# Causal attention and an ELU FFN on one core: first queries of later pairs in float16, and new planner costs

## The chip, the cores and the metric

The kernel runs on one core of a Trainium2 chip. The metric is the device time of one execution in microseconds (us), the median of several runs. The core has five engines with queues of their own: PE (TensorE: matmuls; its weight loads are shown as PEld), DVE (VectorE), ACT (ScalarE), POOL (GpSimd) and SP (SyncE), which here only issues DMAs. Each engine takes its instructions in order. Data lie in SBUF (128 partitions), in PSUM (where PE writes, eight banks) and in DRAM.

## The reference

Attention over 8 batches, 8 heads, 576 positions and 64 dimensions per head, causal, with a decay bias; then a two-layer FFN from 512 over 2048 to 512 with an ELU:

```python
scores = q @ k.T / 8
cum = cumsum(maximum(s, 0))                     # per batch and head
bias = minimum(-(cum[:, None] - cum[None, :]), 0)
scores = where(causal, -1e9, scores + bias)
attn = softmax(scores)                          # with + 1e-9 in the divisor
x = (attn @ v), heads side by side              # 4608 x 512, float32
h = x @ w_in
g = where(h > 0, h, exp(minimum(h, 0)) - 1)
out = g @ w_out                                 # 4608 x 512, float32
```

q, k and v arrive in float32. The two weight matrices arrive as 8-byte floats and are decoded on the chip.

## The kernel before, in words

**A planner.** Nothing is issued in the order in which the code is written. Each step is handed to `op` as a list of ways (engine, cost in ns, the call) with what it reads and writes and a priority. `Plan.issue` then simulates the engines with these costs: again and again it takes the step that could start first (ties go to the lower priority number), on the engine where it would end first, and appends it to that engine's queue. What comes of it is one fixed order for each engine. A load is planned on SP and is taken to land after a transfer time (bytes by `RATE`) and a fixed `LAG`, 4000 ns. `MARGIN` is added where PE depends on another engine. Up to 130 us of planned time the costs and margins are those of the early stage, then the steady ones (`STEADY_T`, `STEADY_BIAS`, `STEADY_MARGIN`). `W0` and `WD` set the priority of the weight units among the attention units: weight unit f has 25 + 3f, the attention units go up in steps of 10 and 5.

**Fillers.** While planned PE time is below `FILL_T` (60 us), gaps of PE are filled with turns of the identity matrix into a scratch bank (line 1556). Nothing reads it. A "turn" is a transposition of a 128x128 tile on PE.

**Attention, first batches.** The first three batches' first 320 positions are computed in float32 by `Low` units, one for each pair of heads (12 units; lines 756 to 895). The two heads' first 64 queries share one 128-row tile (`pair`); the other blocks follow. Probabilities are turned on PE (lines 851 and 867), copied to SBUF, and multiplied with v (lines 853 and 882) into one bank. The pair's product gives 64 rows with 128 columns, one half of them for each head; so the bank is emptied by one copy of 256 columns and two copies of 64 columns that move a head's half to its partitions. Then x goes to DRAM.

**Attention, later pairs.** All other positions use float16 in two parts, high and low (three products instead of one). In five batches each of the four head pairs has a unit with `h is None` for the 64 first queries of both heads, 20 in all, followed by one unit per head. Scores (line 1074) go through DVE with the mask (line 1077) and ACT's Exp (line 1082). For the head units, the normalized probabilities are split into float16 parts (`halved`, lines 1134 to 1142) and turned by a transposing DMA on SP (`turned_load`, line 418). For the first queries the tile stays float32: it is normalized (lines 1095 to 1099), turned on PE (line 1227), evicted into two fp32r parts by a copy and a subtraction (`split_pt`, lines 452 and 1160) and multiplied with an fp32r split of v (line 1220). Four operations (`halves`, lines 452 and 1289) add the diagonal blocks and bring them into x. The heads' products (line 1261) run on halves of the array, one for each head, and are scaled on the way out (lines 1273 and 1275).

**Scales.** Powers of two for the float16 parts come from maxima over all partitions: the per-partition maxima are multiplied with the identity (line 667), reduced on DVE, and spread again by a product with ones (line 670). That happens 13 times.

**FFN.** The 4608 rows of x are taken in 18 chunks of 256. Chunk 0 is computed in float32 (lines 1432 and 1486) while weights arrive; the others use float16 parts (lines 1436 and 1493). A weight unit is a 512 KB load into one of four raw buffers (line 413), an operation on ACT for its high words (line 702), one on DVE or ACT for its low words (lines 706 and 708), one on DVE that joins them (line 711), and a maximum (line 632 or 635). When all 32 are there, the scales are formed and the weights are split (lines 437 to 439 and 726). FFN steps have the priority number 10000 and more on PE, so they fill what attention leaves.

Of the kernel before, what the change touches and what calls it, by code (L numbers as in the profile page):

```python
# [9 lines left out]
F32 = mybir.dt.float32  # L10
F32R = mybir.dt.float32r
# [24 lines left out]
LAG, RATE = 4000.0, 285.0  # L36
W0, WD = 25, 3
# [14 lines left out]
FILL_T, GAP = 60e3, 350.0  # L52
# [44 lines left out]
class Plan:  # L97
# [17 lines left out]
    MARGIN = {"PE": 100.0}  # L115
    STEADY_MARGIN = {"PE": 500.0}

# [82 lines left out]
    def issue(self):  # L200
# [19 lines left out]
        while pending:  # L220
# [144 lines left out]
def kernel(  # L365
# [55 lines left out]
    def rounded(prio, n, dst, src, reads, writes, sign=1.0, only=None):  # L421

        ways = [
            ("Pool", pool_1(n),
             lambda: pool.tensor_scalar(dst(), src(), sign, 1.0, ALU.mult, ALU.mult)),
            ("ACT", act_s(n),
             lambda: act.activation(dst(), src(), AF.Copy, scale=sign)),
            ("DVE-SB", dve_1(n),
             lambda: dve.tensor_scalar(dst(), src(), sign, None, ALU.mult)),
        ]  # L430
        op(prio, [w for w in ways if only is None or w[0] in only], reads, writes)

# [9 lines left out]
    def rest(prio, n, dst, src, hi, reads, writes, only=None):  # L442

        ways = [
            ("DVE-SB", dve_2(n), lambda: dve.tensor_tensor(dst(), src(), hi(), ALU.subtract)),
            ("Pool", pool_2(n), lambda: pool.tensor_tensor(dst(), src(), hi(), ALU.subtract)),
        ]
        op(prio, [w for w in ways if only is None or w[0] in only], reads, writes)
# [36 lines left out]
    def decay_sums():  # L485
# [25 lines left out]
        op(-10, [("DVE-SB", 4390.0, first)], [], [(aux, "row"), (k_first, "sums")])  # L511
# [103 lines left out]

    def scale_tiles():
# [29 lines left out]
    def scales_of(prio, spans, dst):  # L646
# [20 lines left out]
        op(prio, [("PE", pe4(P), lambda: pe_.matmul(flat.v[:, :P], tops.v, ident, start=True, stop=True))],  # L667
# [17 lines left out]
    def load_unit(f, kind, src):  # L685
# [4 lines left out]
        if wide:  # L690
            slot = (2 * f + kind) % N_RAW

            def raw(t):
# [15 lines left out]
                    raw(0), raw(0), AF.Copy, scale=7.49 * 2.0**-32)),  # L709
            ], [], [(raws, (slot, 0))])  # L710
# [131 lines left out]
    def weighing_low(u):  # L842
# [6 lines left out]
        def pair():  # L849
            tr = plan.buf(ps, [P, 512], F32, f"trl_{u.tag}", tag="a", bufs=N_A)  # L850
            op(prio, [("PE", 111.0, lambda: pe_.transpose(tr.v[:, :P], u.first.v, ident))], [u.first], [tr])
            psum_copy(prio, P, lambda: turned.v[:, :P], lambda: tr.v[:, :P], [tr], [(turned, "pair")])
            op(prio, [("PE", pe4(P), lambda: pe_.matmul(
                av.v[:HB, n : n + P], u.vs.v[:, 0], turned.v[:, :P], start=True, stop=True))],
               [(turned, "pair"), u.vs], [av])

        def keys(kb):
# [22 lines left out]
            def products():  # L880
                for h in range(2):
                    pe_.matmul(av.v[h * HB : (h + 1) * HB, n - c : n], u.vs.v[:, 1 + 2 * kb + h], dst()[:, h],
# [147 lines left out]
    def prepare(u):  # L1030
# [17 lines left out]
        src, used = (lambda: u.va.v[:, j, :1]), values_of(u.va, j)  # L1048
# [108 lines left out]
    def split_pt(prio, tag, tr, w):  # L1157
        pc = plan.buf(sb, [P, 2, w], F32R, f"pc_{tag}", tag="pc")
        psum_copy(prio, w, lambda: pc.v[:, 0], lambda: tr.v[:, :w], [tr], [(pc, 0)])
        op(prio, [("DVE", dve_p(w), lambda: dve.tensor_tensor(  # L1160
            pc.v[:, 1], tr.v[:, :w], pc.v[:, 0].bitcast(F32), ALU.subtract))],
           [tr, (pc, 0)], [(pc, 1)])
        return [(pc, 0), (pc, 1)]

    def scoring(u):
# [8 lines left out]
        if u.h is None:  # L1174
            sm = plan.buf(sb, [P, 1], F32, f"sm_{u.tag}", tag="sm", bufs=2)
            psh = u.pp = plan.buf(sb, [P, P], F32, f"psh_{u.tag}", tag="pc")

            def pair():
# [6 lines left out]
                    (sm, 0, True, 1, 1.0), view=lambda v: v.rearrange("p (h t) -> p h t", h=2),  # L1185
                )
                normalize(prio, psh, P, sm, 0)
# [24 lines left out]
    def weighing(u):  # L1212

        prio = u.prio + 1
        av = plan.buf(ps, [P, 512], F32, f"av_{u.tag}", tag="av", bufs=N_AV)

        def products(cost, pairs, dst, first, last):

            for m, (reads, operands) in enumerate(pairs):
                op(prio, [("PE", cost, lambda m=m, operands=operands: pe_.matmul(  # L1220
                    av.v[:, dst], *operands(), start=first and m == 0,
                    stop=last and m == len(pairs) - 1))], reads, [av])
# [439 lines left out]
```

## Time and profile before

| | us |
|---|---|
| three runs | 1029.07, 1031.0, 1031.82 |
| median | 1031.0 |
| profiled execution | 1028.56 |
| its span | 1026.4 |

The span runs from the first to the last instruction of the profile. In what follows, a row of the group view names a line, an engine, an operation, what it writes and reads, its shape and count; then come busy time in us and mean ns of one, then the idle time of the engine before them and what ended it. Rows of the timeline begin with start and duration in us. Matmuls overlap: a row's duration is longer than the distance to the next matmul's start. Rows of the window view show busy us and count of each engine in a stretch, the granted clock of PE, the busy share of the 16 DMA engines and GB/s. `_None` at the end of a tile's name marks the units of the first queries of later pairs; names that end in `l` (`trl`, `avl`, `xl`) belong to the first batches.

### The profile page before, as it was taken

The numbers are of one execution on the slowest core, as the hardware profiler recorded it, in microseconds if no ns is written. First come the engines' busy times: TensorE is split into PE (matmuls) and PEld (weight loads), VectorE is DVE, ScalarE is ACT, GpSimd is POOL, SyncE is SP. The second block draws the span as 40 slices with busy tenths as digits, with TensorE's granted clock in tenths as the row PEclk, the third lists the DMA queues.
The fourth block names the chain that finished last, engine by engine and source line by source line (L and its number), as shares of the span: only waits on it lengthen the run. The fifth ranks groups of instructions, "written<-read, shape, count | busy, mean of one in ns | idle before, by whom it ended". The sixth has DMA issues, their size and how long they took to land. (4 is left out here: it accounts for less than half of the span.)

```text
span 1026.4 us, 21904 instructions
## 1 busy us (share of the span) xinstructions
PE 1005.4 (98%) x7342; PEld 690.3 (67%) x7342; DVE 851.8 (83%) x2394; ACT 661.5 (64%) x1583; POOL 247.0 (24%) x411
## 2 busy tenths in 40 slices
PE   8899999999999999999999999999999999999998
PEld 7666656776666666666666666667666766666665
DVE  6898899888989988889999999898879898763343
ACT  5888746667767777667676777765757666553232
POOL 6231432233232122212422322131212132100000
PEclk9999999999999999999999999999999999999999
DMA  7898324689989998879999999989987998851000
GB/s 204 261 281 258 98 83 129 147 184 238 207 180 190 215 214 186 168 186 230 189 188 207 217 192 192 212 194 202 218 186 178 218 214 177 166 109 48 1 22 21
DMA packets 296725, 179.85 MB, mean 175 GB/s; under 512 B 209908, under 2 KB 270564, under 8 KB 296612
## 3 DMA queue, kind: packets, MB, share of 16 engines
q1 hardware_dynamic: 296612, 178.45, 77.2%
q8 instruction: 58, 0.95, 0.4%
q14 instruction: 55, 0.45, 0.2%
HBM read 93.08 MB, written 36.81 MB: 127 GB/s over the span
## 5 line engine op out<-in xcount | busy, mean ns | idle before, releaser
L1436 PE MATMUL h<-xh,wp 128*128 128x256 f16 x2176 | 398.6, 273 | 0.0
L1493 PE MATMUL o<-wp,gg 128*128 128x512 f16 x1632 | 392.6, 379 | 1.0 <-DVE gg L1475 1.0
L1436 PEld LDWEIGHTS <-wp 128*128 128x128 f16 x3264 | 317.2, 98 | 65.2 <-issue 2.4
L1436 PE MATMUL h<-xl,wp 128*128 128x256 f16 x1088 | 296.5, 273 | 0.7 <-DVE xl L1412 0.7
L1493 PEld LDWEIGHTS <-gg 128*128 128x128 f16 x1632 | 157.9, 98 | 147.1 <-DVE gg L1475 2.9
L1082 ACT ACTIVATE p<-p,mn 128x192 f32<-128x192 f32 (+1 forms) x232 | 143.9, 620 | 65.5 <-DVE mn L1077 59.9
L1142 DVE SCALAR_TENSOR_TENSOR p<-p,sm,p 128x512 f16<-128x512 f32 (+3 forms) x263 | 158.6, 622 | 1.3 <-POOL p L1134 0.3
L1448 ACT ACTIVATE g<-h,cs 128x512 f32<-128x512 f32 x136 | 92.4, 680 | 84.3 <-PE h L1436 83.9
L1472 ACT ACTIVATE gg<-h 128x512 f16<-128x512 f32 x134 | 79.6, 594 | 89.3 <-DVE h L1468 87.8
L1077 DVE CUSTOM_DVE_ANT_0 p<-sc,maskw 128x192 f32<-128x192 f32 (+1 forms) x232 | 109.0, 480 | 11.0 <-PE sc L1074 8.9
L1074 PE MATMUL sc<-set 128*128 128x288 f16 (+3 forms) x544 | 110.8, 298 | 3.3 <-DVE mn L1077 3.2
L1475 DVE SCALAR_TENSOR_TENSOR gg<-h,gg 128x512 f16<-128x512 f32 x136 | 93.2, 686 | 22.8 <-ACT gg L1472 22.1
L1134 POOL TENSOR_SCALAR p<-p,sm 128x64 f16<-128x64 f32 (+3 forms) x77 | 54.2, 707 | 225.9 <-DVE sm L1088 88.8
L1468 DVE SCALAR_TENSOR_TENSOR h<-g,cs,h 128x512 f32<-128x512 f32 x136 | 101.9, 749 | 5.5 <-ACT g L1455 1.4
L1138 ACT ACTIVATE p<-p,sm 128x512 f16<-128x512 f32 (+3 forms) x147 | 78.6, 545 | 18.4 <-ACT p L1082 6.6
L1459 DVE TENSOR_SCALAR g<-g 128x512 f32<-128x512 f32 x98 | 43.2, 441 | 55.2 <-ACT g L1448 54.8
L1074 PEld LDWEIGHTS <-set 128*128 128x128 f16 x584 | 54.7, 98 | 37.8 <-issue 6.0
L1261 PEld LDWEIGHTS <-v 128*64 128x64 f16 x960 | 48.2, 110 | 21.3 <-issue 11.9
L1261 PE MATMUL av<-T,v 128*64 128x256 f16 (+5 forms) x960 | 61.4, 278 | 0.8 <-DMA T<-p 0.8
L437 POOL TENSOR_SCALAR v<-va,scales 128x320 f16<-128x320 f32 (+1 forms) x35 | 24.2, 691 | 115.2 <-PE av L1261 92.7
L437 POOL TENSOR_SCALAR xh<-xc,cs 128x512 f16<-128x512 f32 x23 | 17.3, 753 | 112.8 <-PE h L1436 104.6
L1082 ACT ACTIVATION_READ_ACCUMULATOR p<-p,mn 128x1 f32 x232 | 43.6, 188 | 0.0
(202 smaller groups left out, 1264.0 us busy)
## 6 DMA issues: line engine op xcount, KB each, us to landing
set<-spread SPq DMA_DIRECT2D x32, 432.0 KB
spread<-parts_None SPq DMA_DIRECT2D x32, 288.0 KB
set<-spread SPq DMA_DIRECT2D x32, 288.0 KB
raws<-in_w_in_dram SPq DMA_DIRECT2D x16, 512.0 KB
raws<-in_w_out_dram SPq DMA_DIRECT2D x16, 512.0 KB
out_dram<-ost SPq DMA_DIRECT2D x32, 256.0 KB
va<-in_vb_dram SPq DMA_DIRECT2D x16, 352.0 KB
xc<-x_dram SPq DMA_DIRECT2D x22, 256.0 KB
```

The source lines that it names most:

```text
L1074: pe_.matmul(view(sc.v[:, :cw]), l, r, start=n == 0, stop=n == len(pairs) - 1)
L1077: op(prio, [("DVE", 168 + cw + 55 * (i > 0), lambda i=i, sc=sc: dve.tensor_tensor_reduce(pt.v[:, i * cw : (i + 1) * cw], sc.v[:, :cw], mv( ...
L1082: op(prio, [("ACT", 383 + w / 1.2, lambda: act.activation(pt.v[:, :w], pt.v[:, :w], AF.Exp, bias=mn.v[:, n - 1 : n], scale=-1.0, accum_out ...
L1138: ("ACT", 295 + size / 1.2, lambda part=part: act.activation(part(0), own(part), AF.Copy, scale=sm.v[:, r])),
L1142: ("DVE-SB", dve_2(size), lambda part=part: dve.scalar_tensor_tensor(part(1), own(part), sm.v[:, r], part(0), ALU.mult, ALU.subtract)),
L1261: pe_.matmul(av.v[w.h * HB : (w.h + 1) * HB, dst], w.values.v[:, w.h, kb, v], part(w, kb, m), start=kb == 0 and m == 0 and v == 0, stop=kb ...
L1436: pe_.matmul(columns(k), weight_part(f, 0, part)[1]()[:, c * P : (c + 1) * P], xx.v[:, c], start=(c == 0 and m == 0), stop=(c == NCB - 1 a ...
L1448: op(side, [("ACT", act_c(W) + (0 if native else 90), lambda: act.activation(g.v, hp.v, AF.Exp, scale=1.0 if native else by(3)))], [hp] + ...
L1468: op(side, [("DVE", dve_p(W) + 60, lambda: dve.scalar_tensor_tensor(hp.v, g.v, by(2 if sign[0] else 1), hp.v, ALU.mult, ALU.max))], [g, cs ...
L1472: ("ACT", act_c(W), lambda: act.activation(gg.v[:, 0], hp.v, AF.Copy, scale=2.0**-DOWN)),
L1475: op(side, [("DVE", dve_p(W), lambda: dve.scalar_tensor_tensor(gg.v[:, 1], hp.v, 2.0**-DOWN, gg.v[:, 0], ALU.mult, ALU.subtract))], [hp, ( ...
L1493: pe_.matmul(acc[i].v, gg.v[:, g, at], weight_part(f, 1, part)[1](), start=(f == 0 and m == 0), stop=(f == NF - 1 and m == 2),)
```

## The change

Later pairs' first queries: the probabilities are scaled by 2^15 over their sum and split into two float16 parts (`split_scaled`: a scaled copy on POOL, ACT or DVE, then the remainder on DVE), and both parts go through one transposing DMA of two blocks. The values of these queries are split into float16 parts as well. The products are six matmuls of 64 columns, one head on each half of the array; they stand in `heads` of the pair's second head, ahead of its products, share its bank and eviction where these fit in 512 columns (batch 3), and have a bank and an eviction of 64 columns of their own elsewhere.

First batches: the pair's product is made for each head on its half of the array, with 64 columns, so that the bank is emptied by one copy of 320 columns. The decoding of low words may also run on POOL. The scales' turns use the transposition of PE. An Exp on ACT is added near the start. Planner values change: `LAG` is 2300 plus 300 early and 1700 later, `W0` 22, the early margin of PE 50, `FILL_T` 42 us, and the first scan's cost 3100 ns.

```diff
-LAG, RATE = 4000.0, 285.0
-W0, WD = 25, 3
+LAG, RATE = 2300.0, 285.0
+W0, WD = 22, 3
-FILL_T, GAP = 60e3, 350.0
+FILL_T, GAP = 42000.0, 350.0
...
-    MARGIN = {"PE": 100.0}
+    MARGIN = {"PE": 50.0}
     STEADY_MARGIN = {"PE": 500.0}
+    EARLY_LAG, STEADY_LAG = 300.0, 1700.0
...
-                lag = pipe + o.ways[n][3] - end
+                lag = pipe + o.ways[n][3] + (self.STEADY_LAG if steady else self.EARLY_LAG) - end
...
+    def split_scaled(prio, n, dst, src, by, used, parts):
+        scaled(prio, n, lambda: dst(0), src, by, used, [(parts, 0)])
+        op(prio, [("DVE-SB", dve_2(n), lambda: dve.scalar_tensor_tensor(
+            dst(1), src(), by(), dst(0), ALU.mult, ALU.subtract))], [*used, (parts, 0)], [(parts, 1)])
...
-        op(-10, [("DVE-SB", 4390.0, first)], [], [(aux, "row"), (k_first, "sums")])
+        op(-10, [("DVE-SB", 3100.0, first)], [], [(aux, "row"), (k_first, "sums")])
...
+    def first_exp():
+        o = op(-30, [("ACT", 1500.0, lambda: act.activation(junk[:, :1], ident[:, :1], AF.Exp))])
...
-        op(prio, [("PE", pe4(P), lambda: pe_.matmul(flat.v[:, :P], tops.v, ident, start=True, stop=True))],
+        op(prio, [("PE", 111.0, lambda: pe_.transpose(flat.v[:, :P], tops.v, ident))],
            [tops], [flat])
...
+                ("Pool", pool_1(512), lambda: pool.tensor_scalar(
+                    raw(0), raw(0), 2.0**-29, 7.0, ALU.mult, ALU.min)),
...
-            op(prio, [("PE", pe4(P), lambda: pe_.matmul(
-                av.v[:HB, n : n + P], u.vs.v[:, 0], turned.v[:, :P], start=True, stop=True))],
-               [(turned, "pair"), u.vs], [av])
+            def products():
+                for h in range(2):
+                    pe_.matmul(av.v[h * HB : (h + 1) * HB, :HB], u.vs.v[:, 0], turned.v[:, h * HB : (h + 1) * HB],
+                               start=True, stop=True)
+            op(prio, [("PE", pe4(HB), products)], [(turned, "pair"), u.vs], [av])
...
-            psum_copy(prio, n, lambda: x.v[:, HB:LOW], lambda: av.v[:, :n], [av], [(x, 2)])
-            for h in range(2):
-                rows, a0 = slice(h * HB, (h + 1) * HB), n + h * HB
-                psum_copy(prio, HB, lambda rows=rows: x.v[rows, :HB],
-                          lambda a0=a0: av.v[:HB, a0 : a0 + HB], [av], [(x, h)])
+            psum_copy(prio, LOW, lambda: x.v[:, :LOW], lambda: av.v[:, :LOW], [av], [x])
...
-        u.vs = plan.buf(sb, [P, 1, 2, D], F32R, f"vs_{u.tag}", tag="vs0", bufs=NP)
+        u.vs = plan.buf(sb, [P, 2, D], F16, f"vs_{u.tag}", tag="vs0", bufs=NP)
...
-        rounded(prio, D, lambda: u.vs.v[:, :1, 0], src, used, [u.vs])
-        rest(prio, D, lambda: u.vs.v[:, :1, 1], src,
-             lambda: u.vs.v[:, :1, 0].bitcast(F32), used, [u.vs])
+        by = lambda: scales.v[:, u.col : u.col + 1]
+        split_scaled(prio, D, lambda m: u.vs.v[:, m], src, by, used, u.vs)
...
+            p16 = plan.buf(sb, [P, 2, P], F16, f"ph_{u.tag}", tag="ph")
+            u.pt = plan.buf(sb, [P, 2, P], F16, f"th_{u.tag}", tag="th", bufs=2)
...
-                normalize(prio, psh, P, sm, 0)
+                split_scaled(prio, P, lambda m: p16.v[:, m], lambda: psh.v, lambda: sm.v[:, :1],
+                             [sm, (psh, "data")], p16)
+                turned_load(prio, 2, lambda: u.pt.v, lambda: p16.v.rearrange("p m q -> p (m q)"),
+                            [(p16, 0), (p16, 1)], [u.pt])
...
-        if u.h is None:
-            def pair():
-                tr = plan.buf(ps, [P, 512], F32, f"tr_{u.tag}", tag="a", bufs=N_A)
-                op(prio, [("PE", 111.0, lambda: pe_.transpose(tr.v[:, :P], u.pp.v, ident))],
-                   [(u.pp, "data")], [tr])
-                pieces = split_pt(prio, u.tag, tr, P)
...
-                for h in range(2):
-                    halves(prio, h, HB, u.x_part((h, 0)), 0, av, h * HB)
...
+        front = u.front if not first else None
+        c0 = HB * (front is not None and wq + HB <= 512)
...
+            if front is not None:
+                fav = av if c0 else any_bank(f"avh_{u.tag}")
+                def front_step():
+                    for m, v in ((0, 0), (1, 0), (0, 1)):
+                        for h in range(2):
+                            pe_.matmul(
+                                fav.v[h * HB : (h + 1) * HB, :HB], front.vs.v[:, v], front.pt.v[:, m, h * HB : (h + 1) * HB],
+                                start=m == 0 and v == 0, stop=v == 1,
+                            )
+                op(prio, [("PE", 120.0, front_step)], [front.pt, *[(w.pt, i) for w in pair for i in u.blocks],
+                                                       (front.vs, 0), (front.vs, 1)], [fav])
+                if not c0:
+                    evicted(HB, lambda: x.v[:, :HB], lambda: fav.v[:, :HB], [fav], [(x, "first")])
...
+    first_exp()
     decay_sums()
```

More of the change, by code (lines that the diff above doesn't have):

```diff
@@ L419, in turned_load @@
                    units * P * P * 2.2)], reads, writes)
[L421 to L431, printed above, removed]
     def scaled(prio, n, dst, src, by, reads, writes):
@@ L881, in products @@
                 for h in range(2):
[L882 removed]
+                    pe_.matmul(av.v[h * HB : (h + 1) * HB, LOW - c : LOW], u.vs.v[:, 1 + 2 * kb + h], dst()[:, h],
                                start=kb == 0, stop=kb == CUT)
@@ L1214, in weighing @@
         prio = u.prio + 1
[L1215 to L1222, printed above, removed]
-        if u.h is None:
-            def pair():
-                tr = plan.buf(ps, [P, 512], F32, f"tr_{u.tag}", tag="a", bufs=N_A)
-                op(prio, [("PE", 111.0, lambda: pe_.transpose(tr.v[:, :P], u.pp.v, ident))],
-                   [(u.pp, "data")], [tr])
-                pieces = split_pt(prio, u.tag, tr, P)
-                products(pe(P), [
-                    ([pc, u.vs], lambda pc=pc, m=m: (
-                        u.vs.v.rearrange("p n a d -> p n (a d)")[:, 0], pc[0].v[:, m]))
-                    for m, pc in enumerate(pieces)], slice(P), True, True)
-                for h in range(2):
-                    halves(prio, h, HB, u.x_part((h, 0)), 0, av, h * HB)
-            return [pair]
-        if u.h == 0:
+        if u.h != 1:
             return []
         pair = (u.first_head, u)
+        av = plan.buf(ps, [P, 512], F32, f"av_{u.tag}", tag="av", bufs=N_AV)
         first, last, wq = u.blocks[0], u.last + 1, P * u.n_blocks
+        front = u.front if not first else None
+        c0 = HB * (front is not None and wq + HB <= 512)
         def columns(kb):
@@ L1255, in heads, with evicted @@
         def heads():
+            x, label = u.x_part(("rows", first))
+            back = slice(u.back, u.back + 1)
+            def evicted(n, dst, src, reads, writes):
+                op(prio, [
+                    ("ACT", act_c(n) + 90, lambda: act.activation(dst(), src(), AF.Copy, scale=scales.v[:, back])),
+                    ("DVE", dve_p(n), lambda: dve.tensor_scalar(dst(), src(), scales.v[:, back], None, ALU.mult)),
+                ], [*reads, (scales, u.back)], writes)
+            if front is not None:
[11 more added lines that the diff above has]
+                    evicted(HB, lambda: x.v[:, :HB], lambda: fav.v[:, :HB], [fav], [(x, "first")])
             def step():
                 for kb in range(last + 1):
-                    dst = slice(wq - columns(kb), wq)
+                    dst = slice(c0 + wq - columns(kb), c0 + wq)
                     for m, v in ((0, 0), (1, 0), (0, 1)) if kb < last else ((0, 0), (0, 1)):
@@ L1269, in heads @@
                [av])
[L1270 to L1277 removed]
+            cols = slice(HB + P * first - c0, HB + P * first + wq)
+            evicted(c0 + wq, lambda: x.v[:, cols], lambda: av.v[:, : c0 + wq], [av], [(x, label)])
             load(prio, lambda: x_dram.v[u.b, u.j][:, u.cols], lambda: x.v[:, u.cols], [x],
@@ L1319, in attention @@
                 if u.h == 0:
-                    first_head = u
+                    first_head, u.front = u, None if u.blocks[0] else front
+                u.front = first_head.front
                 u.first_head = first_head
+            if type(u) is Unit and u.h is None:
+                front = u
             prepared(u)
```

35 lines of the change are left out of this document (3 added, 32 removed).

## The prediction

> **What bounds the kernel now.** I read the page first: its busy times and its clock, then the chain of waits. All times are in us.
>
> ```profile
> span 1026.4 us, 21904 instructions
> PE 1005.4 (98%) x7342; PEld 690.3 (67%) x7342; DVE 851.8 (83%) x2394; ACT 661.5 (64%) x1583; POOL 247.0 (24%) x411
> PEclk9999999999999999999999999999999999999999
> PE 15%; DVE 1%; ACT 0%; issue 0%; DVEq 0%
> ```
>
> PE is busy 98% of the span, the granted clock is full throughout, and the chain, as far as it can be followed back, is matmuls behind matmuls. But a mean hides stages, so next come the windows of the whole kernel, and the window of line 1556 alone, the fillers (turns of the identity into a scratch bank that no one reads).
>
> ```profile
> 0.00:60.00 60.00, 53.98 (x372) 42.01 (x372) 47.11 (x144) 43.24 (x133) 25.82 (x67) 1.00 0.82 236
> 60.00:115.00 55.00, 53.04 (x288) 36.15 (x286) 49.05 (x163) 46.92 (x143) 14.13 (x37) 1.00 0.85 254
> sum 700.00, PE 692.43 PEld 473.42 DVE 627.42 ACT 479.98 POOL 177.28; mean PE 98.92 PEld 67.63 DVE 89.63 ACT 68.57 POOL 25.33
> ...
> 0.00:60.00 60.00, 23.68 (x176) 22.05 (x176) 1.00 0.82 236
> ```
>
> Columns are PE, PEld, DVE, ACT, POOL, the clock, the share of the DMA engines, GB/s. From 170 to 870 (the sum line) PE is 98.9% busy and DVE 89.6%: a microsecond of PE removed there should come off the end. In the first 60, however, 23.7 of PE's 54.0 are fillers. That stage waits for loads, softmax and weight decoding, and whatever shortens it moves all that follows forward, as long as PE stays the bound behind it.
>
> **The change, later pairs (steady stage).** Twenty pair units (five batches of four head pairs) lose one TensorE turn, two products, two evictions of the turned tile and four operations that assemble x. The groups by form and the timeline of PE:
>
> ```profile
> L1220 PE MATMUL av_None<-pc_None,vs_None 128*128 128x128 f32 x40 | 9.8, 318 | 0.0
> L1227 PE MATMUL tr_None<-ident,psh_None 128*128 128x128 f32 x20 | 5.8, 288 | 1.8 <-POOL psh_None L1095 1.4 <-DVE psh_None L1097 0.2 <-ACT psh_None L1099 0.2
> L1261 PE MATMUL av<-T,v 128*64 128x64 f16 x144 | 8.4, 194 | 0.0
> ...
> 42.43 0.49 PE L1556 MATMUL scratch<-ident 128*128 128x128 f32 x3
> 42.76 0.38 PE L867 MATMUL trl<-ident,p 128*128 128x128 f32 x2
> ...
> 191.06 0.83 PE L1261 MATMUL av<-T,v 128*64 128x256 f16 x16
> 191.82 0.28 PE L1436 MATMUL h<-xh,wp 128*128 128x256 f16 x1
> ...
> 192.92 0.27 PE L1436 MATMUL h<-xl,wp 128*128 128x256 f16 x1
> 193.03 0.27 PE L1436 MATMUL h<-xh,wp 128*128 128x256 f16 x1
> 193.06 0.42 PE L1220 MATMUL av_None<-pc_None,vs_None 128*128 128x128 f32 x2
> 193.32 0.28 PE L1436 MATMUL h<-xh,wp 128*128 128x256 f16 x1
> ```
>
> Durations overlap, so I price by starts. A turn: three in 42.76 - 42.43 = 0.33, so 0.11 each, 2.2 for twenty. Its waits: 1.8, by the idle column. The products: from one ordinary matmul to the next 0.29 instead of 0.11, so 0.18, 3.6 for twenty. Removed: 7.6. Added: six products of 64 columns on half the array for each unit. The 16 products from 191.06 stream (6x256 + 6x192 + 4x64)/2 = 1472 columns in 0.76; six of 64 are 192 columns, so 0.10 when they stand next to these. The highest price is that of the 64-column group: 8.4 over 72 pairs is 0.117, three pairs 0.35. Twenty cost 2.0 to 7.0; I take 2.5, because both steps become ready by the same turned tiles and have one priority, so the planner should set them side by side. Net -5.1 (bounds -5.6 and -0.6).
>
> [...]
>
> The scale turns at line 667 become real turns:
>
> ```profile
> L667 PE MATMUL flat<-ident,tops 128*128 128x128 f32 x26 | 5.3, 287 | 0.2 <-ACT tl L452 0.2
> L1160 DVE TENSOR_TENSOR pc_None<-tr_None,pc_None 128x128 fp32r<-128x128 f32 x20 | 5.7, 285 | 0.1
> L1289 DVE TENSOR_TENSOR x_None<-av_None,x_None 64x64 f32<-64x64 f32 x40 | 8.7, 219 | 1.9 <-ACT x_None L452 1.4
> L1142 DVE SCALAR_TENSOR_TENSOR p<-p,sm,p 128x64 f16<-128x64 f32 x59 | 18.0, 305 | 0.1
> L1142 DVE SCALAR_TENSOR_TENSOR p<-p,sm,p 128x256 f16<-128x256 f32 x44 | 23.8, 552 | 0.4 <-POOL p L1134 0.3
> ```
>
> The 13 products are 26 passes there, while the 20 turns above are 20: one pass of 0.11 saved each. Eight of them lie in the steady stage, -0.9. Together -6.0.
>
> DVE gives up 5.7 + 8.7 = 14.4 (and some copies) and gets a low half of 128 columns, between 0.305 and 0.552, say 0.39, and one of 64 for the values, 0.305: 20 x 0.70 = 13.9. ACT gives up copies of the turned tile and of x, more than the one eviction of 64 columns that sixteen units add. I count both at nothing: PE's own queue of work hides them, and without that cover they would still be a gain of half a microsecond. In those sixteen units the front products take a bank of their own from the two of the scores or the one of the heads; before, the turn and its products took one of each, so nothing is charged here either.
>
> **The added transfers.** Twenty transposing DMAs of two 128x128 blocks join SP's queue. The rows: the present ones, the matmuls that wait for them, and the queue from 470 to 670.
>
> ```profile
> L418 SPq DMA_TRANSPOSE T<-p x168: 1203/1318/4976, 177.1 to 913.0; - x168
> ...
> L1261 PE MATMUL av<-T,v 128*64 128x256 f16 (+5 forms) x960 | 61.4, 278 | 0.8 <-DMA T<-p 0.8
> ...
> DMA packets 79557, 40.24 MB, mean 201 GB/s; under 512 B 63273, under 2 KB 73189, under 8 KB 79533
> q1 hardware_dynamic: 79533, 39.95, 96.8%
> ```
>
> SP is held 20 x 1.32 = 26 over some 450, and each issue waits there for DVE's low half; what stands behind it on SP is the next pair's q and k, the spread copies and the loads of x. In DMA time, by bytes: 40 blocks of 32 KB are 1.3 MB of 39.95 in 193.6, 6.3. By packets: if each row of 256 B in a block is one, 128 in a block, 5120 of 79533, 12.5. I lean to the packets (most here are under 512 B). The 168 transposes of today cost PE 0.8 in all, so I charge 0, and keep a loss up to 12.5 for a rival.
>
> [...]
>
> **The early stage.** The planner orders by costs; the change lowers the first scan from 4390 to 3100 ns, the early lag of a load from 4000 to 2300 + 300 (steady: 2300 + 1700, as before), starts weights one step earlier and ends fillers at 42 of planned time. The timeline of the start:
>
> ```profile
> 2.85 0.61 SPq L413 DMA_DIRECT2D low_queries<-in_qT_dram  x1
> 5.41 0.38 DVE L502 TENSOR_SCALAR kl_first<-aux 1x320 f32<-1x320 f32 x1
> 10.48 2.12 PE L1074 MATMUL sc<-kl_first,low_queries 128*128 128x128 f32 x10
> 11.12 1.03 DVE L515 TENSOR_SCALAR aux<-aux 64x576 f32<-64x576 f32 x1
> 14.59 0.65 SPq L413 DMA_DIRECT2D kl<-aux  x1
> 16.57 0.61 SPq L413 DMA_DIRECT2D raws<-in_w_in_dram  x1
> ...
> L706 DVE TENSOR_SCALAR raws<-raws 128x512 uint32<-128x512 uint32 x31 | 13.4, 436 | 0.0
> L452 ACT COPY xl<-avl 64x64 f32<-64x64 f32 x15 | 3.1, 204 | 0.8 <-issue 0.4 <-DVE xl L453 0.3
> ```
>
> The sums are ready at 5.79, yet PE begins scores at 10.48, behind a run of fillers; L515 stands behind these scores on DVE, and behind L515 the keys of the second unit and the first weight. The new costs pull this by 1.29 + 1.40 = 2.7; the sums would allow 10.48 - 5.79 = 4.7. I take 2.7. An earlier Exp on ACT is part of it. Relief besides: L706's 13.4 may move to POOL (busy 40 of the first 115); a third is 4.5. The low outputs save two copies of 64 columns at 0.204 per unit less the wider one, about 0.33, 4 over twelve units. ACT and DVE are 81% busy there, so of 8.5 on two engines I let 1.3 reach the end. Early: -4.0; bounds +2 (late loads) and -13 (4.7 and half of 17.4).
>
> **The sum.** The profiled execution took 1028.56 (span 1026.4, 2.2 around it). 1028.56 - 6.0 - 4.0 = 1018.6. The median of the three runs, 1031.0, lies 2.4 above it: 1021.
>
> **The rivals.**
> *Early gain stays behind.* The DMA share is 0.82 to 0.85 until 115, and weights may stay bound by transfers, or POOL may never be picked for the low words, so that the change doesn't do what it says. Only -6.0: 1025. Against it: those 23.7 of fillers.
> *Early gain is large.* DVE and ACT are the true bound of the first 115. With -12 there: 1031 - 18 = 1013. Against it: the same transfers.
> *Gain swallowed.* DVE is at 89.6%, PE waits elsewhere for it: 1030.
> *Slower: transfers.* From 470 to 670 the queue is 96.8% busy, 6.4 of 200 free; 12.5 spread over 450 put 5.6 there, just inside. It decides as soon as the new tiles' transfers end after PE reaches them, for the front products then hold the heads' products and the FFN's matmuls behind them in PE's order. Then the stage takes the transfers' 12.5, the 6.0 is lost, the start keeps 4: 1031 + 8.5 = 1039.5, at half that lateness 1036, which I take. Against it: 0.8 above.
> *Slower: the clock.* With no fillers after 42 PE pauses in a stage that it now runs through (the last row is line 1556 alone):
>
> ```profile
> 42.00:62.00 20.00, 17.71 (x121) 12.42 (x120) 18.61 (x62) 17.12 (x54) 5.58 (x14) 1.00 0.97 273
> 58.88 1.36 PE L1556 MATMUL scratch<-ident 128*128 128x128 f32 x11
> 61.54 0.33 PE L851 MATMUL trl<-ident,pl 128*128 128x128 f32 x1 [1.30 <-ACT pl L1099]
> ...
> 42.00:62.00 20.00, 5.56 (x40) 4.65 (x40) 1.00 0.97 273
> ```
>
> If the granted clock halved there, the real matmuls (17.7 less the 5.6 of line 1556 in the last row) would take as long again, 12: 1031 + 12 - 6 = 1037. Against it: the longest pause without fillers would be 61.54 - 58.88 = 2.7.
>
> [...]
>
> **How the numbers follow.** Forecast (1021, own range 1015 to 1026) 0.42; early stays behind 0.22; early large 0.17; swallowed 0.08; transfers 0.08; clock 0.03. About 0.3% (3.1) can be told from no change. Faster: 0.41 + 0.19 + 0.17 = 0.77; same: 0.10; slower: 0.13. The range takes all but the two slower ones and the far end of the large gain: 1009 to 1034.
>
> **What would show it.** Right: line 1227 and 1220 gone, 188 transposes in place of 168 and no wait for them on PE; the six products next to the heads' at 0.10; first scores near 7.8; chunk 1 beginning some 4 earlier than now. Wrong: PE idle before the heads' products, a granted clock under 1.00 before 70, first weights still at 16.6, or DVE no less busy before 115. A time above 1028 would refute the steady part.

## The result: slower by 1.3%, against a forecast of 1.0% faster

The changed kernel took 1043.62 us (median; 1042.47 to 1044.15), the kernel before 1030.52 beside it: a ratio of 1.0126 with an interval of 1.0108 to 1.0144. The predicted 1021 had the wrong sign, and 1043.6 lies outside its range. The profiled execution took 1043.97 (span 1042.2) against 1028.56 (span 1026.4).

From the page of the changed kernel:

```profile
span 1042.2 us, 21853 instructions
PE 1000.5 (96%) x7349; PEld 680.6 (65%) x7349; DVE 846.4 (81%) x2349; ACT 648.0 (62%) x1529; POOL 269.4 (26%) x401
PEclk9899999999999999999999999999999999999999
```

PE is busy 4.9 us less (1005.4 before), yet the span is 15.8 longer, so PE stands idle 20.7 more. The 4.9 are not a saving of work: the fillers alone fell from 24.2 to 16.75 us, and some of the real matmuls ran at half clock (below). POOL has 22 us more work. The clock row is no longer all nines. The windows say where the idle time lies (columns: PE, PEld, DVE, ACT, POOL, clock, DMA share, GB/s). First the kernel before, cut at 150 and 910:

```profile
0.00:150.00 150.00, 140.52 (x787) 99.84 (x788) 129.73 (x390) 109.83 (x316) 56.50 (x123) 1.00 0.68 199
150.00:910.00 760.00, 752.43 (x5757) 515.28 (x5756) 677.81 (x1934) 517.86 (x1213) 189.08 (x286) 1.00 0.90 193
```

Then the changed kernel: the same two, the two of the start that the prediction showed, the first of these for the fillers alone (line 1537 here; PE and PEld only), and the sum of the seven windows from 170 to 870.

```profile
0.00:150.00 150.00, 132.79 (x759) 94.50 (x760) 130.03 (x394) 115.48 (x328) 87.79 (x135) 0.97 0.77 212
150.00:910.00 760.00, 740.56 (x5684) 500.23 (x5683) 661.76 (x1855) 490.38 (x1130) 180.23 (x265) 1.00 0.89 190
...
0.00:60.00 60.00, 50.61 (x326) 38.16 (x326) 49.07 (x145) 41.49 (x128) 35.72 (x69) 0.94 0.83 227
60.00:115.00 55.00, 48.43 (x292) 33.97 (x290) 47.91 (x155) 47.10 (x141) 31.99 (x44) 0.97 0.96 262
...
0.00:60.00 60.00, 16.75 (x113) 15.55 (x113) 0.94 0.83 227
...
sum 700.00, PE 682.17 PEld 461.98 DVE 610.16 ACT 457.51 POOL 167.99; mean PE 97.45 PEld 66.00 DVE 87.17 ACT 65.36 POOL 24.00
```

Idle time of PE: 9.5 to 17.2 in the first 150, 7.6 to 19.4 from there to 910. Of the 7.7 more in the first 150, some 7.4 are only fillers that are no longer there; that this stage became worse all the same shows in the weights (next paragraphs), which are ready 10 us later. The steady stage lost more: between 170 and 870 PE is busy 97.5% instead of 98.9%, and DVE is *less* busy than before. Nothing has become the new bound by its work; something arrives late.

**The start.** Groups of the changed kernel, and the timeline where PE makes its longest early pause (rows between those shown are left out, here and in the timelines below):

```profile
L701 POOL TENSOR_SCALAR raws<-raws 128x512 uint32<-128x512 uint32 x16 | 35.1, 2195 | 1.4
L704 DVE SCALAR_TENSOR_TENSOR wa<-raws 128x512 uint32<-128x512 uint32 x32 | 22.5, 702 | 5.7 <-POOL raws L701 5.2 <-ACT raws L693 0.2
```

```profile
23.82 7.68 POOL L701 TENSOR_SCALAR raws<-raws 128x512 uint32<-128x512 uint32 x3
26.41 0.69 DVE L704 SCALAR_TENSOR_TENSOR wa<-raws 128x512 uint32<-128x512 uint32 x1 [0.83 <-POOL raws L701]
28.97 0.69 DVE L704 SCALAR_TENSOR_TENSOR wa<-raws 128x512 uint32<-128x512 uint32 x1 [1.15 <-POOL raws L701]
29.69 0.69 DVE L623 TENSOR_REDUCE peaks<-wa 128x1 f32<-128x512 f32 x1
30.50 0.35 DVE L1069 CUSTOM_DVE_ANT_0 p<-sc,maskw 128x192 f32<-128x192 f32 x1
30.73 0.66 PE L864 MATMUL trl<-ident,p 128*128 128x128 f32 x2 [3.40 <-DVE mn L1069]
```

Half of the 32 low words went to POOL, at 2.2 us each; DVE's way took 0.436 and the planner's cost for POOL is 255 + 0.87 x 512 = 700 ns. DVE stands in its own order at the join (L704) until POOL is through (0.83 and 1.15 us here), behind the join stand L623 and the mask (L1069), and for the mask waits PE: 3.40 us of pause. So POOL's lateness is part of this pause; the rest is DVE's own weight work ahead of the mask. The last join ended at 125.5 instead of 115.3, and chunk 1's first matmul came at 153.6 instead of 145.9.

During or after such pauses the granted clock fell. It did so three times before the last microseconds, at 28.18, 82.80 and 488.98, by pauses of 3.40, 2.54 and 2.72. The windows on both sides of the first two falls, and of one in a run below that orders the kernel before anew (5 ns of planned margin):

```profile
24.77:28.18 3.41, 1.51 (x10) 1.01 (x8) 2.19 (x3) 2.04 (x4) 3.33 (x2) 1.00 0.88 237
28.18:35.01 6.83, 4.28 (x16) 3.19 (x16) 4.53 (x16) 3.72 (x12) 4.18 (x4) 0.50 0.89 270
79.39:82.80 3.41, 0.87 (x10) 0.49 (x9) 3.38 (x8) 3.20 (x10) 3.08 (x6) 1.00 1.10 186
82.80:86.21 3.41, 3.41 (x24) 2.77 (x23) 2.31 (x9) 0.66 (x2) 0.90 (x2) 0.50 1.09 255
...
15.36:18.77 3.41, 1.64 (x9) 1.17 (x9) 3.07 (x14) 2.73 (x10) 0.00 (x0) 1.00 0.70 168
18.77:22.18 3.41, 3.41 (x13) 2.78 (x12) 1.55 (x5) 1.46 (x5) 0.00 (x0) 0.50 1.03 341
```

The clock stood at 0.5 for 3.4 or 6.8 us, 13.6 in all. Matmuls went at half the pace there: pairs of turns at line 864 start 0.43 apart at 85.13, 0.22 apart at 77.85. So at most 6.8 of work was lost, by my estimate half of the 13.6. The profile of the kernel before shows no such fall in its span. The falls lie 54.62 and 406.18 apart, 16 and 119 times 3.413, and last once or twice 3.41. In the 3.41 us ahead of them PE was idle for 1.90, 2.54 and 2.18 (3.41 less the PE column). In the run with the margin of 505 ns it was 1.77, by a pause of 1.84. The pause of 2.23 at 739 lay across the border of two such stretches, counted on from the falls, with 1.25 and 1.07 idle in them, and nothing fell; of the changed kernel's other stretches at full clock, up to 1038, the one from 871.27 had the most idle time, 1.61, and nothing fell behind it either. What sets the clock, no run tried apart.

**The steady stage.** Waits of PE from 150 on (total, times, longest), first the largest of the kernel before, then the largest of the changed kernel and two of its timelines:

```profile
PE sc L1074 <- DVE mn L1077: 3.2, 6, 1.2
```

```profile
PE sc L1066 <- DVE mn L1069: 9.0, 11, 2.7
PE av L1254 <- DMA T<-p: 3.1, 3, 1.4
PE sc L1066 <- DMA set<-spread: 3.0, 4, 1.6
```

```profile
222.63 1.32 SPq L419 DMA_TRANSPOSE T<-p  x1
229.60 0.57 PE L1254 MATMUL av<-T,v 128*64 128x256 f16 x8 [1.36 <-DMA T<-p]
```

```profile
483.48 0.65 SPq L414 DMA_DIRECT2D stq_None<-in_qT_dram  x1
...
488.17 0.75 DVE L623 TENSOR_REDUCE pk_None<-stq_None 128x1 f32<-128x576 f32 x1 [3.09 <-DMA stq_None<-in_qT_dram]
489.52 0.64 PE L1066 MATMUL sc<-set 128*128 128x288 f16 x2 [2.72 <-DVE mn L1069]
```

A turned tile issued at 222.63 is used at 229.60, 7.0 later, and PE stood 1.36 for it. A load of q took 4.7 from issue to its use on DVE; DVE stood 3.09 at it, with a mask behind it, and PE stood 2.72 for the mask. The wait list says "DVE", but where this wait is followed back it is a transfer that was late in DVE's order; the others of that row were not all followed back.

PE never stood before the new products. The view of the tile th_None:

```profile
L1239 PE MATMUL avh<-th_None,vs_None x96: 196/196/218, 268.8 to 643.4; 128*64 128x64 f16 x96
...
L419 SPq DMA_TRANSPOSE th_None<-ph_None x20: 1173/1204/2172, 168.3 to 610.9; - x20
its engine sat idle before it (us, times) until:
who waited for it (us, times):
  POOL vs_None L426: 39.8, 11
...
```

The list of what PE waited for before these products is empty. The waits in the last rows are those for the products to end: POOL waits there to write the next pair's values. So the new transfers, if they cost anything, cost it to others.

### The profile page after: what moved, and what is told of

It reads as the page before. It is cut to its first block, busy times and chain, and to the rows that moved or that the text cites. A ratio compares the mean times of both kernels' runs of the same rounds, so it can differ in the third digit from the quotient of the medians.

```text
span 1042.2 us, 21853 instructions
## 1 busy us (share of the span) xinstructions
PE 1000.5 (96%) x7349; PEld 680.6 (65%) x7349; DVE 846.4 (81%) x2349; ACT 648.0 (62%) x1529; POOL 269.4 (26%) x401
## 2 busy tenths in 40 slices
DMA packets 302485, 181.16 MB, mean 174 GB/s; under 512 B 215668, under 2 KB 276324, under 8 KB 302372
## 3 DMA queue, kind: packets, MB, share of 16 engines
q1 hardware_dynamic: 302372, 179.76, 77.6%
## 5 line engine op out<-in xcount | busy, mean ns | idle before, releaser
L1474 PEld LDWEIGHTS <-gg 128*128 128x128 f16 x1632 | 157.9, 98 | 145.9 <-DVE gg L1456 1.7
L1134 DVE SCALAR_TENSOR_TENSOR p<-p,sm,p 128x512 f16<-128x512 f32 (+3 forms) x263 | 154.3, 611 | 8.0 <-ACT p L1130 6.5
L1126 POOL TENSOR_SCALAR p<-p,sm 128x512 f16<-128x512 f32 (+3 forms) x76 | 54.8, 723 | 242.3 <-DVE sm L1080 99.0
L1069 DVE CUSTOM_DVE_ANT_0 p<-sc,maskw 128x192 f32<-128x192 f32 (+1 forms) x232 | 109.0, 480 | 8.0 <-PE sc L1066 4.8
L1130 ACT ACTIVATE p<-p,sm 128x64 f16<-128x64 f32 (+3 forms) x155 | 81.9, 535 | 28.0 <-DMA T<-p 9.5
L1254 PEld LDWEIGHTS <-v 128*64 128x64 f16 x960 | 49.7, 110 | 21.3 <-issue 13.1
L426 POOL TENSOR_SCALAR v<-va,scales 128x320 f16<-128x320 f32 (+1 forms) x37 | 21.1, 575 | 94.7 <-PE av L1254 76.6
```

The costliest lines, as they stand in the source:

```text
L1069: op(prio, [("DVE", 168 + cw + 55 * (i > 0), lambda i=i, sc=sc: dve.tensor_tensor_reduce(pt.v[:, i * cw : (i + 1) * cw], sc.v[:, :cw], mv( ...
L1130: ("ACT", 295 + size / 1.2, lambda part=part: act.activation(part(0), own(part), AF.Copy, scale=sm.v[:, r])),
L1134: ("DVE-SB", dve_2(size), lambda part=part: dve.scalar_tensor_tensor(part(1), own(part), sm.v[:, r], part(0), ALU.mult, ALU.subtract)),
L1254: pe_.matmul(av.v[w.h * HB : (w.h + 1) * HB, dst], w.values.v[:, w.h, kb, v], part(w, kb, m), start=kb == 0 and m == 0 and v == 0, stop=kb ...
L1474: pe_.matmul(acc[i].v, gg.v[:, g, at], weight_part(f, 1, part)[1](), start=(f == 0 and m == 0), stop=(f == NF - 1 and m == 2),)
```

## The experiments

Ratios are to the kernel before on the same chip, with a 95% interval.

**Undoing parts, with the planner at work.** Four kernels, each planned anew.

The changed kernel without POOL's way for the low words:

```diff
-                ("Pool", pool_1(512), lambda: pool.tensor_scalar(
-                    raw(0), raw(0), 2.0**-29, 7.0, ALU.mult, ALU.min)),
```

> The changed kernel without the new way for low words on GpSimd (DVE and ACT as before). Theory A, the GpSimd decode costs the early stage: the profile after shows 16 of the 32 low words on GpSimd at 2.2 us each where the planner counts 0.70, and the last weight joined 10 us later than before; without it that join comes back to about 115 us, chunk 1 begins near 145 and the time falls by 6 to 10, to 1034 to 1038. Rival B, the early deficit is caught up by 307 us in the profile after (chunk 3 ends at the same time in both), so the end is set by the steady stage: the time stays at 1041 to 1045.

1.0219 (1.0191 to 1.0246): slower than the whole change, though POOL's 35 us are gone.

All new operations, but old planner values, no POOL way (removed as above), no early Exp:

```diff
-LAG, RATE = 2300.0, 285.0
-W0, WD = 22, 3
-FILL_T, GAP = 42000.0, 350.0
-    MARGIN = {"PE": 50.0}
-    EARLY_LAG, STEADY_LAG = 300.0, 1700.0
+LAG, RATE = 4000.0, 285.0
+W0, WD = 25, 3
+FILL_T, GAP = 60e3, 350.0
+    MARGIN = {"PE": 100.0}
+    EARLY_LAG, STEADY_LAG = 0.0, 0.0
...
-        op(-10, [("DVE-SB", 3100.0, first)], ...
+        op(-10, [("DVE-SB", 4390.0, first)], ...
...
-    first_exp()
```

> All operations of the change (float16 front products, DMA turns, one copy of the first batches' outputs, the scales' turns), but with the planner's values of before, no early Exp and no low words on GpSimd. If the prediction's steady part was right and only the new values and the GpSimd way cost time: -6 for the steady stage, 1022 to 1028. If the added transfers cost the steady stage (stalls of PE behind late DMAs between 450 and 870 us): 1036 to 1044.

1.0150 (1.0119 to 1.0182). The kernel before with the new planner values alone (the same lines the other way, without the Exp):

> The kernel before with the planner's new values alone (lag, W0, early margin, fillers until 42, scan cost). If the shorter early lag and fewer fillers are what lets PE pause and the granted clock fall: 1034 to 1042 and a granted clock under 1.00 before 90 us. If they help, as predicted for the early stage: 1026 to 1029.

1.0096 (1.0074 to 1.0117). Both parts alone are slower, by 15.5 and 9.9 us of 1031; the whole, which also has POOL's way and the Exp, is 13.0. They don't add up. And the changed kernel with fillers until 60 again:

```diff
-FILL_T, GAP = 42000.0, 350.0
+FILL_T, GAP = 60e3, 350.0
```

> The changed kernel with fillers until 60 us of planned time as before. If missing fillers cause the half clock at 28 to 35 and at 80 us: clock 1.00 there and 3 to 6 faster, 1038 to 1041. If PE's in-order waits do it (the pause of 3.7 us at 27 lies before 42 us, inside the fillers' reach): no difference, 1042 to 1045.

1.0142 (1.0114 to 1.0170): no gain, and the clock still falls in the first 60 (0.91 there). The planner set 134 filler turns, against 113 in the changed kernel and 177 before, so not all came back; but the pause at 27 to 31 lies inside the fillers' reach in both runs and is still there (3.61 us). Missing fillers are not its cause; a gap that arises on the chip is not one that the planner saw.

**Does the order alone move the time?** Two edits of planner values that change no operation, on the kernel before and one of them on the changed one:

```diff
-    HOP = 35.0
+    HOP = 36.0
```

> The kernel before with one planner constant moved by 1 ns (HOP, the assumed delay between two engines, 35 to 36): no operation changes, only the order that the planner draws. Theory A, the order of before was a fortunate draw and any edit loses it: pauses of PE over 1.5 us and half clock appear as in the changed kernel, 1036 to 1050. Rival B, the change's own operations cost the time: this stays at 1029 to 1034 with no pause over 1.5 us.

1.0022 (1.0006 to 1.0039).

```diff
-    STEADY_MARGIN = {"PE": 500.0}
+    STEADY_MARGIN = {"PE": 505.0}
```

> A second such draw of the kernel before (the steady margin of PE 500 to 505 ns, so the early stage keeps its order). Theory A: 1036 to 1050, with the loss behind 150 us alone. Rival B: 1029 to 1034.

1.0081 (1.0056 to 1.0106) on the kernel before.

> The same nudge on the changed kernel (500 to 505 ns). Theory A: the steady part is redrawn, so anything from 1030 to 1055, with other pauses at other places. Rival B: 1042 to 1045, with the pauses at the same work.

1.0139 (1.0104 to 1.0174) on the changed one. Five nanoseconds of planned margin cost the kernel before 0.8%. Its waits of PE behind 150 with that order:

```profile
PE sc L1074 <- DVE mn L1077: 7.1, 9, 1.6
PE av L1261 <- DMA T<-p: 2.0, 2, 1.8
```

These are the kinds of waits of the changed kernel. So a run that replans says little about the part it undoes: the order changes with it. This is why the four runs above settle nothing by themselves.

**Is it the planned lag of a load?** The two transfers followed above took 4.7 and 7.0 us from issue to use, where the planner counts transfer plus 4.0. One microsecond more in the steady stage:

```diff
-    EARLY_LAG, STEADY_LAG = 300.0, 1700.0
+    EARLY_LAG, STEADY_LAG = 300.0, 2700.0
```

> The changed kernel with the planner's steady lag of a load raised by 1000 ns (4000 to 5000). If PE's steady pauses come from transfers that land later than planned (in the profile after, four of the six pauses over 1.3 us go back to a DMA issued 5 to 7 us before the data were there): fewer pauses behind 150 us, 7 to 12 instead of 17, no half clock there, and 1032 to 1040. If lateness is not the cause: 1042 to 1052.

1.0014 (0.9998 to 1.0029): 11.5 us of the loss gone, though one steady pause of 3.47, with half clock, is left at 365. The same microsecond on the new operations with old values, and on the kernel before:

> All operations of the change with the early planner values of before, no early Exp, no low words on GpSimd (the kernel that took 1047.5), and the steady lag raised by 1000 ns to 5000. If late transfers made that kernel slow: 1024 to 1033, with fewer pauses behind 150 us than its 22.8 and no half clock there. If the lag helped the changed kernel only by a lucky order: 1040 to 1050.

1.0080 (1.0064 to 1.0097).

> The kernel before with its steady lag raised by 1000 ns to 5000 and nothing else. If its order at 4000 already meets few late transfers (7.6 us of pauses behind 150 us), the larger lag only spreads the plan: 1031 to 1042. If any order gains by the lag: 1024 to 1029.

1.0182 (1.0148 to 1.0216): here it costs 18 us. The two largest of PE's waits of this kernel behind 150:

```profile
PE sc L1075 <- DVE mn L1078: 10.1, 13, 4.3
PE sc L1075 <- DMA set<-spread: 3.3, 3, 1.6
```

One microsecond more still on the changed kernel (3700), and 2700 with the margin of 505:

> The changed kernel with the steady lag at 6000. If lateness sets the steady pauses, they fall further or stay low (below 10 us), and the time is 1028 to 1038; if more lag costs buffers and room on PE, 1038 to 1050 with few pauses for DMA but more attention left behind for the end.

1.0064 (1.0048 to 1.0080).

> A second order of the changed kernel with the steady lag of 5000: the steady margin of PE at 505 ns as in the run that took 1045.5. If the lag is what repaired the changed kernel: 1031 to 1038 again. If the first was a lucky order: 1040 to 1048.

0.9975 (0.9962 to 0.9988), 1028.26 us: the whole change in another order is faster than both kernels, with the sum of its windows from 170 to 870 and the largest of its waits behind 150:

```profile
sum 700.00, PE 693.55 PEld 470.26 DVE 616.50 ACT 464.05 POOL 154.29; mean PE 99.08 PEld 67.18 DVE 88.07 ACT 66.29 POOL 22.04
```

```profile
PE sc L1066 <- DVE mn L1069: 5.5, 5, 3.2
```

A larger lag is no cure in itself, since it cures one kernel and harms the other. Taken together, the operations of before were run in five orders, 1.000 to 1.0182; the changed ones, with and without POOL's way, in nine, 0.9975 to 1.0219. The two ranges overlap for most of their width, so these runs do not show that the new operations are slower in a typical order.

**One cost taken away, in the same order.** In these runs every engine keeps the order of the kernel that they start from: the step stays in the plan with its planned cost, only its call is replaced. (The traces bear it out: apart from the replaced calls and a constant tile set at the start, the instructions of each engine come in the same order.) POOL clears the low words instead of decoding them (this leaves out the three lowest bits of half of the weights):

```diff
-                ("Pool", pool_1(512), lambda: pool.tensor_scalar(
-                    raw(0), raw(0), 2.0**-29, 7.0, ALU.mult, ALU.min)),
+                ("Pool", pool_1(512), lambda: pool.memset(raw(0), 0)),
```

> The changed kernel in exactly its own order on every engine, but the 16 low words on GpSimd are only cleared (left out: three low bits of these weights). Theory: the decode there takes 2.2 us and more where 0.70 is planned, PE pauses at 27 and 80 us behind it, and the granted clock halves; cleared in 0.6 to 0.8 us each, the pauses at 27 and 80 fall under 1.5, the clock stays 1.00 until 100, chunk 1 begins near 146 instead of 153.6, and the time is 1035 to 1039. Rival: the early deficit is made up later in any case (at 307 us both kernels had equal progress): 1041 to 1045 with an earlier chunk 1.

1.0078 (1.0049 to 1.0107): 4.9 us off the 13.0, and chunk 1 begins at 150.3 instead of 153.6. The early pauses did not go under 1.5 as expected: PE still stands 2.66 at 30 and 2.00 at 80, behind DVE's work, and the clock is 0.97 in both early windows. So POOL's decode lengthens these pauses but does not make them. The source view of the clearing:

```profile
L701 POOL MEMSET raws<- x16: 548/568/677, 25.1 to 117.5; 128x512 uint32 x16
```

The twenty new transfers left out (the front products read a constant tile, set once on POOL, so the first 64 queries of later pairs are not computed):

```diff
-                turned_load(prio, 2, lambda: u.pt.v, ...
+                op(prio, [("SP", 1330.0, lambda: None, LAG, 2 * P * P * 2.2)], ...
...
-    ... front.vs.v[:, v], front.pt.v[:, m, h * HB : (h + 1) * HB],
+    ... front.vs.v[:, v], steady_pt[:, m, h * HB : (h + 1) * HB],
```

> The changed kernel in its own order without the 20 new transposing DMAs (left out: the first queries' products read a constant tile in place of the turned probabilities). Theory transfers: these 20 take SP 26 us and the DMA engines 6 to 12, and what queues behind them is late; without them the steady pauses fall from 17 to 10 or less and the time is 1030 to 1037. Rival, the order: the late transfers are those of the old kinds (T, stq, va, set) and stay late: 1040 to 1045.

0.9999 (0.9985 to 1.0012): 13.1 us off. The window from 150 to 910, and PE's waits behind 150:

```profile
150.00:910.00 760.00, 751.05 (x5798) 509.20 (x5798) 674.19 (x1887) 499.48 (x1149) 181.61 (x265) 1.00 0.89 191
```

```profile
PE sc L1068 <- DVE mn L1071: 4.5, 6, 2.0
...
PE sc L1068 <- DMA set<-spread: 1.2, 4, 0.3
PE av L1255 <- DMA T<-p: 0.6, 1, 0.6
```

Until 150 PE's idle time does not change (17.2 in both); from there to 910 it falls from 19.4 to 8.9, that is 10.5 of the 13.1. The three waits shrink by half or more: 9.0 to 4.5, 3.0 to 1.2, 3.1 to 0.6. Both taken away:

> Both of these at once, same order. If the two costs are separate they add: what the first and the second gain, together. If all that is left is the order: still above 1033.

0.9940 (0.9911 to 0.9969): the transfers are worth 14.2 with POOL cleared (13.1 without), the decode 6.1 without transfers (4.9 with). The two costs add, within intervals of 2.4 to 4.2 us either way, and without them this kernel is 6.2 us faster than before; it leaves out work, so this is not a time that the change could reach as it stands. In the better order (2700, 505) the cleared words again:

> The fastest order so far (the changed kernel with steady lag 5000 and margin 505, 1028.3) with the same clearing of the low words on GpSimd, order unchanged. If the decode costs the early stage 5 to 7 us and PE is the bound behind it: 1021 to 1024, the predicted time. If the early deficit is made up later: 1026 to 1029.

0.9911 (0.9882 to 0.9939), 6.6 us (0.0064 of 1031) below the same order with the decode; chunk 1 begins at 146.5 instead of 154.9. That its 1021.3 us are the forecast's number is chance: the order is another, the decode is left out, and the transfers that the forecast took as free are in it.

**What of a transfer costs it?** In the order of the changed kernel, the front products on the constant tile as above, each of the twenty transposing DMAs becomes a plain copy, first of one partition, then of all:

```diff
+    ("SP", 1330.0, lambda: nc.sync.dma_start(u.pt.v[:1], p16.v[:1]), ...     one partition
+    ("SP", 1330.0, lambda: nc.sync.dma_start(u.pt.v, p16.v), ...             all 128
```

> The changed kernel in its own order, each of the 20 new transposing DMAs replaced by a plain copy of one partition (512 bytes) that waits on SP for the same tiles (left out: the first queries' products read a constant tile). If SP's waits for the low half in the middle of its queue cost the 13 us that go without these DMAs: 1039 to 1045. If the cost lies in the transposing transfers themselves: 1029 to 1034.

> The same with a plain copy of the whole 64 KB in place of each transposing DMA (the products still read the constant tile). If bytes on the DMA engines cost the time: near the changed kernel, 1039 to 1045. If only the transposing form does (more packets, a longer issue): 1029 to 1034.

1.0048 (1.0030 to 1.0065) and 1.0053 (1.0032 to 1.0075). The issues of the first in the view of th_None (nanoseconds: least, median, most), and SP's wait for them:

```profile
L1177 SPq DMA_DIRECT2D th_None<-ph_None x20: 559/594/672, 169.1 to 609.2; - x20
...
SPq L1177 <- DVE sm L1082: 8.9, 2, 8.3
```

In the second the median is 546. The 64 KB themselves cost nothing that can be told (0.5 us between the two, intervals overlapping). About 5 of the 13 come with any DMA at this place. That SP stands there in its order until DVE has the low half is not the reason: in the traces of these two runs and of the changed kernel it stands long only before the first of the twenty (some 8 us, ahead of 170), and the other nineteen start 0.1 after the issue before them. What is left is the time that each issue holds SP, 0.55 to 0.59, with all later loads behind it. The other 7.5 to 8 come with the transposing form; it holds SP 1.20, which is 12 to 13 us more of SP's queue in some 440. All three fit a loss of about half a microsecond for each microsecond that SP is held (5.0 for 11.9, 5.6 for 10.9, 13.1 for 24.1; twenty times the median). But the transposing form also makes more packets: by the profiles' pages, the DMA queue of the changed kernel has 302372 instead of 296612, 5760 more, where the copy of 64 KB adds 2880 and that of one partition 640. How much of the 7.5 is SP's queue and how much the transposition in the DMA engines was not tried apart.

## Why the prediction was wrong, step by step

**"So I charge 0", for the added transfers: the step that failed.** They cost 13.1 to 14.2 in this order; in the order that took 0.9975 they are there too, and no run took them out of it. I had priced them by what today's 168 transposes cost PE directly (0.8), and looked for the price where the new tile is used. There nobody waits. The price falls on the others in SP's queue and behind them: from the kernel before to the changed one, PE's wait for the turned tiles of other pairs grew from 0.8 to 3.1, that for the spread copies from nothing to 3.0, and that for masks (the "DVE mn" wait; DVE stands at a load with the mask behind it) from 3.2 to 9.0, and without the transfers they shrink again. That each issue waits for DVE's low half, as I wrote, was wrong for nineteen of the twenty. I named these ("what stands behind it on SP") and gave them no price. The rival *Slower: transfers* was nearest, with 1036 to 1039.5, but its mechanism was another: it let the new tiles come after PE reaches them, and it let bytes and packets decide. (Nor does its 1036 follow: half of 8.5 gives 1035, half of the 12.5 alone less the 4 gives 1033.) One row or 64 KB made no difference, so the 6.3 by bytes was not the cost. My count of 5120 packets was right (5760 more, of which the copy of one partition adds 640 as well), but whether they cost anything is open, as said above. Plain copies in the same places made the kernel 6 us faster (1043.6 to 1037.6), though those runs' products don't wait for them.

**"L706's 13.4 may move to POOL", counted as relief: wrong in sign.** POOL was picked (16 of 32, 35 us), so the move happened, and it cost 4.9 to 6.6 in three comparisons. The missing question was what POOL needs for this operation: the trace before has no such row, and the prediction gave POOL no price at all. The join on DVE waits in order, so a slow way off the path is put onto it. Of the early -4.0 little is left: first scores came 1.5 earlier (8.99 instead of 10.48, forecast 7.8), but the first weight's load still stood at 16.6, and chunk 1 began at 153.6, 7.7 later instead of some 4 earlier. With the decode gone it begins at 150.3 in this order and at 146.5 in the other, never before the 145.9 of the kernel before. What else holds the start back has no run of its own.

**Front products side by side at 2.5: too low.** Sixteen of twenty got a bank of their own, and all but one of these stand apart from the heads' products, among matmuls of the FFN and the scores; only four share the heads' bank:

```profile
268.59 0.27 PE L1417 MATMUL h<-xh,wp 128*128 128x256 f16 x1
268.80 0.28 PE L1239 MATMUL avh<-th_None,vs_None 128*64 128x64 f16 x6
269.01 0.28 PE L1417 MATMUL h<-xh,wp 128*128 128x256 f16 x1
```

From one h to the next 0.42 instead of 0.11: 0.31 for each of the sixteen. The four beside the heads' products take 0.12 (at 227.85, heads' products from 227.97). 16 x 0.31 + 4 x 0.12 = 5.4, inside my bounds of 2.0 to 7.0 but twice my value. So a step that stands alone cost 0.31, and one beside the heads' products, which run on halves of the array as it does, 0.12; what makes the difference no run tried apart. "One priority and ready together" did not make the planner set them together. The steady gain in PE's work is then 7.6 - 5.4 + 0.9 = 3.1, not 6.0.

**What held.** Lines 1227 and 1220 are gone, there are 188 transposes, and the scale turns and DVE's low half cost about what I said:

```profile
L658 PE MATMUL flat<-ident,tops 128*128 128x128 f32 x13 | 3.9, 299 | 3.5 <-DVE tops L647 3.5
L434 DVE SCALAR_TENSOR_TENSOR ph_None<-psh_None,sm_None,ph_None 128x128 f16<-128x128 f32 x20 | 9.3, 466 | 0.3 <-POOL ph_None L426 0.2
```

Thirteen single passes instead of 26; 0.466 instead of 0.39. DVE's work before 115 stayed (96.2 to 97.0), which I had listed as a sign against me. With both failed terms taken out in the same order, the change gave -6.2 (interval -9 to -3) where the sum said -10; the mis-sized term of the products (3.1 instead of 6.0) and the missing early gain are of the size of that difference, though no run separates them.

**The clock.** I put a pause of 2.7 against this rival, and nothing that I had read in the traces showed how long a pause may be. Here half clock came with pauses of 3.40, 2.54 and 2.72, and in another order with one of 1.84, while one of 2.23 passed without it. In these cases the idle time within 3.41 us tells the falls (1.77 and more) from the rest (1.61 and less); the length of one pause does not. The rival's cause, too few fillers, is not borne out: with fillers planned until 60 again the pause and the fall stayed. The fall is a second cost of the pauses, at most 6.8 us here by the estimate above.

**An assumption I never wrote down:** that the rest of the order stays. The sum adds and removes terms in a fixed schedule, but any edit may have the planner draw a new one, and for the same operations that alone moved the time by 0.2 to 1.8%. The kernel before sits in a good order, by luck or by earlier tuning: its four neighbours with the same operations are all slower. The same change in another order is 0.25% faster than before. What makes an order good is not settled; more lag helps one and harms the other.

## What to carry to other kernels

When a planner fixes the order of in-order queues, don't judge an edit by replanned variants alone: keep the order and replace one call at a time, which here gave two costs that add up. Price a DMA also by what stands behind it in its issuing queue, not only by who waits for its data, and price a new way on another engine by a measured row of that very operation before the planner may choose it. If two or three harmless edits of a planner value move the time by as much as the change promises, the forecast needs a range of that size.

## What the runs showed of the hardware

POOL's uint32 multiply-and-minimum over 128x512 took 2.0 to 2.5 us, where DVE took 0.44 and POOL's clear of the same words 0.57. The granted clock fell to 0.5 for 3.4 or 6.8 us in the changed kernel, each time after a stretch of 3.41 us in which PE had been idle for 1.90 to 2.54, so never for all of it; in one other run it came after 1.77 of 3.41. An SP issue of a two-block transpose held the queue 1.20 us, a plain copy of the same 64 KB 0.55. A load of 128 KB and a turned tile were used 4.7 and 7.0 us after their issue, while the DMA share was 1.03 and 1.08.
